# A recurrent attention feeding a gated MLP: attention one chunk ahead instead of two, second product two steps behind, a fixed activation table set with Ln ahead of the Exp, and an own order of units for the first three steps

## Chip, cores, metric

The kernel runs on one core of one Trainium2 chip. The metric is the device time of one execution in microseconds (us). The kernel before takes 262.17 us, the median of four runs (260.22 to 262.91).

## The reference

Gated linear attention over 768 positions (4 batches, 8 heads, head size 48), and its output as the input of an MLP whose gate is h·cos(h):

```python
for t in range(S):                                  # attention, per batch and head
    state = alpha[:, :, t, :, None] * state + einsum('bhd,bhe->bhde', k[:, :, t], v[:, :, t])
    y[:, :, t] = einsum('bhd,bhde->bhe', q[:, :, t], state)
x = y.transpose(0, 2, 1, 3).reshape(3072, 384)
h = x @ w_in                                        # 384 -> 2048, "ff1" below
out = (h * np.cos(h)) @ w_out                       # 2048 -> 384, "ff2" below
```

## The kernel before

The 3072 rows are worked through in 24 chunks of 128 rows (six per batch). The order of instructions on each engine is the order in which the program writes them; nothing reorders them afterwards. The decay is handled through logarithms: Ln of alpha, a cumulative sum on TensorE ("cums"), then two Exp. This is done for two chunks at a time. The cosine is a Sin with bias pi/2. Units, with the engine of each:

- Per pair of chunks: `ln` (ACT), `cums` (PE), `exps` (two Exp, ACT).
- Attention of a chunk: `operands` (GpSimd), `transposes` (PE, "T"), `ev_transposes` (DVE), `state` (PE, "S") and its eviction (DVE), `scores` (PE) and their masking (DVE), `outputs` (PE) and `ev_outputs` (DVE).
- MLP of a chunk, in two halves: `ff1` (PE), `act` (Sin, ACT), `gate` (multiply, DVE), `ff2` (PE), and the eviction of the result (ACT).

PSUM holds eight banks. Three two-bank buffers ("big") go round among ff1, scores and cums. One bank ("g") goes round among transposes, state and outputs, so each of these three waits until DVE has evicted the one before. One bank ("o") holds ff2's result.

```python
    def load_w1(f0, f1): ...
    def cast_w1(f0, f1):
        nc.scalar.activation(out=w1[:, 0:2, f0:f1], in_=w1f[:, 0:2, f0:f1], func=AF.Copy)
        nc.vector.tensor_copy(out=w1[:, 2, f0:f1], in_=w1f[:, 2, f0:f1])
    def cast_w2(f):
        nc.vector.tensor_copy(out=w2[:, f : f + 8], in_=w2f[:, f : f + 8])
    ...
    def prep(g):
        cums(2 * g, 2)
        exps(2 * g, 2)
        if 2 * g + 2 < NCH:
            ln(2 * g + 2, 2)

    nc.scalar.preload_act_table_set("natural_log_exp_and_others")
    load_a(0); load_qk(0); load_v(0); load_a(1)          # written on lines of their own
    load_w1(0, DF // 2)
    load_qk(1); load_v(1)
    load_w1(DF // 2, DF)
    load_a(2); load_a(3)
    ...                                                   # more loads; chunks 0 to 2 of the attention
    for s in range(NCH + 1):
        ...                                               # loads
        if s + 3 < NCH: operands(s + 3, nc.gpsimd)
        if s + 2 < NCH: transposes(s + 2); ev_transposes(s + 2)
        if s < NCH:     ff1(s, 0); t0 = act(s, 0)
        if s + 2 < NCH: state(s + 2); ev_state(s + 2)
        if s < NCH:     gate(s, 0, t0)
        if s == 0:      cast_w1(DF // 2, DF)
        if s == 1:      cast_w2(0); cast_w2(8)            # a loop in the source
        if s >= 1:      ff2(s - 1, 0)
        if s < NCH:     ff1(s, 1); t1 = act(s, 1)
        if s + 1 < NCH: outputs(s + 1); ev_outputs(s + 1)
        if s < NCH:     gate(s, 1, t1)
        if s >= 1:      ff2(s - 1, 1); ev_ff2(s - 1)
        if s + 2 < NCH: scores(s + 2); mask_scores(s + 2)
        if s % 2 == 0 and s + 4 < NCH:
            prep(s // 2 + 2)
```

## Time and profile before

| | before |
|---|---|
| time, median of four | 262.17 us |
| span of the profiled run | 260.2 us |
| PE busy | 211.3 us |
| ACT / DVE / GpSimd busy | 135.6 / 136.1 / 62.6 us |
| start of step 2 (its transposes) | 57.4 us |
| three pairs of steps, mean (103.42 to 159.64 us, between first matmuls of cums) | 18.74 us |

The page of the kernel before: the engines' busy time with share of the span and number of instructions, and the clock granted to TensorE in 40 slices of 6.5 us, in tenths.

```profile
PE 211.3 (81%) x2625; PEld 155.4 (60%) x2626; DVE 136.1 (52%) x160; ACT 135.6 (52%) x144; POOL 62.6 (24%) x104
...
PEclk9775779689999979999999999999999989999998
```

PE is the busiest engine, and it is idle 19% of the time. The clock is lower in most of the start (slices 2 to 9) and again in slices 15 and 33.

The timeline of the kernel before over one boundary of a pair. Columns: start in us, duration in us, engine, line, operation, output and input with shapes, count; in brackets the idle time of the engine before it and what ended it. L161 and L163 are the two Exp, L131 is Ln, L311 Sin, L316 the gate, L287 the eviction of the attention's outputs, L192 the transposes.

```profile
122.97 1.28 ACT L161 ACT_TABLE_LOAD   x1 [0.49 <-PE cum_new L148]
...
124.97 0.81 ACT L163 ACTIVATE cp_new<-cum_new 128x776 f32<-128x776 f32 x1
...
125.81 1.28 ACT L131 ACT_TABLE_LOAD   x1
...
127.10 0.84 ACT L131 ACTIVATE lnab<-a_new 128x768 bf16<-128x768 f32 x1
...
127.96 1.28 ACT L311 ACT_TABLE_LOAD   x1
...
129.25 2.12 ACT L311 ACTIVATE c_sb<-t,halfpi 128x1024 bf16<-128x1024 f32 x2
...
130.40 1.22 DVE L316 TENSOR_TENSOR g_new<-t,c_sb 128x1024 bf16<-128x1024 f32 x1 [4.70 <-ACT c_sb L311]
...
131.54 0.55 DVE L287 CAST t<-t 128x384 bf16<-128x384 f32 x1
...
132.14 0.38 PE L192 MATMUL t<-ident_bf,khb 128*128 128x128 bf16 x4 [1.55 <-DVE t L287]
```

Read it from top to bottom as one chain. After the cums ACT loads a table, does two Exp, loads a second table for Ln, does Ln, loads a third for Sin, and only then starts the Sin of an ff1 that PE had finished long before. The gate on DVE waits 4.70 us for it. The output eviction, whose input was ready, stands behind that gate in DVE's order, and PE's transposes wait 1.55 us for the bank that it frees.

The table of waits of the kernel before, PE only, 57 to 225 us: who waited for whom, total us, number, longest.

```profile
PE t L192 <- DVE t L287: 14.6, 8, 2.3
PE t L232 <- DVE t L198: 5.5, 6, 0.9
```

Both waits together are 20.1 us, which is all of PE's idle time in this stretch (168.0 us, PE busy 147.9). L232 is the state product, L198 the eviction of the transposes.

PE in the start of the kernel before:

```profile
27.46 2.64 PE L302 MATMUL t<-t,w_112 128*128 128x128 bf16 x24
...
49.91 2.72 PE L325 MATMUL o_new<-w_114,g_new 128*128 128x384 bf16 x8 [7.99 <-DVE w_114 L125]
...
57.41 0.40 PE L192 MATMUL t<-ident_bf,khb 128*128 128x128 bf16 x4
```

The first ff1 matmul (L302) runs at 27.46 us. The first ff2 matmul (L325) waits 7.99 us for the cast of w2. Step 2 starts at 57.41 us.

### The profile page before, as it was taken

The page shows a single profiled execution, that of the slowest core. Times are in us where ns is not written, and L with a number is a line of the kernel's source. Part 1 is how long each engine was busy: PE and PEld are TensorE (multiplying, and loading weights), DVE is VectorE, ACT ScalarE, POOL GpSimd, SP SyncE. Part 2 cuts the span into 40 slices and gives each one's busy share as a digit, 9 for nine tenths or more (in the row PEclk, how much of TensorE's full clock was granted, in tenths as well). Part 3 has the DMA queues.
Part 4 walks back from the last instruction along what each step waited for, and adds up shares of the span by engine and source line. Part 5 has one row for each costly group of instructions (what it writes and reads, how often), then busy time and mean ns, then how long its engine had stood idle before and what let it go on. Part 6 is the DMA issues. An engine that isn't in the chain of part 4 may idle for free. (4 is left out here: it accounts for less than half of the span.)

```text
span 260.2 us, 6131 instructions
## 1 busy us (share of the span) xinstructions
PE 211.3 (81%) x2625; PEld 155.4 (60%) x2626; DVE 136.1 (52%) x160; ACT 135.6 (52%) x144; POOL 62.6 (24%) x104
## 2 busy tenths in 40 slices
PE   7661673399969969969969869879789699999994
PEld 2430562176846856847747557567567487676762
DVE  6450234845465266276186185276366456765540
ACT  4323657123863943953944925916836736523440
POOL 3121215610420610610700700701602502500000
PEclk9775779689999979999999999999999989999998
DMA  8999999907734843743762671664355140000001
GB/s 142 314 300 188 347 238 179 197 5 154 152 74 84 155 99 53 154 107 60 141 133 59 115 151 41 113 146 93 69 123 116 39 92 33 33 2 31 33 30 62
DMA packets 106203, 30.28 MB, mean 116 GB/s; under 512 B 100288, under 2 KB 105408, under 8 KB 106176
## 3 DMA queue, kind: packets, MB, share of 16 engines
q1 hardware_dynamic: 106176, 29.89, 54.0%
q8 instruction: 20, 0.33, 0.5%
q14 instruction: 7, 0.06, 0.1%
HBM read 25.17 MB, written 4.72 MB: 115 GB/s over the span
## 5 line engine op out<-in xcount | busy, mean ns | idle before, releaser
L311 ACT ACTIVATE c_sb<-t,halfpi 128x1024 bf16<-128x1024 f32 x48 | 52.5, 1112 | 71.2 <-PE t L302 71.1
L316 DVE TENSOR_TENSOR g_new<-t,c_sb 128x1024 bf16<-128x1024 f32 x48 | 58.5, 1218 | 49.9 <-ACT c_sb L311 49.9
L302 PE MATMUL t<-t,w_112 128*128 128x128 bf16 x1152 | 77.4, 227 | 3.2 <-ACT w_112 L115 3.2
L325 PE MATMUL o_new<-w_114,g_new 128*128 128x384 bf16 x384 | 71.9, 332 | 8.6 <-DVE w_114 L125 8.0
L302 PEld LDWEIGHTS <-w_112 128*128 128x128 bf16 x1152 | 72.4, 103 | 6.9 <-ACT w_112 L115 3.5
L173 POOL TENSOR_TENSOR khb<-t,icp_new 128x384 bf16<-128x384 f32 x24 | 24.2, 1008 | 154.6 <-ACT icp_new L161 131.5
L325 PEld LDWEIGHTS <-g_new 128*128 128x128 bf16 x384 | 36.0, 99 | 32.0 <-issue 10.7
L287 DVE CAST t<-t 128x384 bf16<-128x384 f32 x24 | 13.3, 554 | 32.8 <-PE t L261 32.8
L218 DVE TENSOR_TENSOR t<-t,mask_f 128x1024 bf16<-128x1024 f32 x24 | 29.3, 1220 | 1.8 <-PE t L209 1.2
L244 DVE TENSOR_TENSOR t<-t,Em 128x384 bf16<-128x384 f32 x24 | 13.4, 558 | 21.1 <-PE t L238 18.9
L330 ACT ACTIVATE o_sb<-o_new 128x384 f32<-128x384 f32 x24 | 11.8, 490 | 23.3 <-PE o_new L325 23.3
L175 POOL TENSOR_TENSOR qhb<-t,cp_new 128x384 bf16<-128x384 f32 x22 | 23.4, 1062 | 0.6 <-DMA t<-in_q_dram 0.6
L192 PE MATMUL t<-ident_bf,khb 128*128 128x128 bf16 x96 | 9.6, 223 | 17.1 <-DVE t L287 14.6
L198 DVE COPY t<-t 128x1024 bf16<-128x1024 bf16 x24 | 16.4, 682 | 9.9 <-PE t L192 9.9
L261 PE MATMUL t<-t 128*64 128x128 bf16 (+1 forms) x160 | 20.8, 231 | 0.0
L261 PE MATMUL t<-t,vpb 128*64 128x128 bf16 x288 | 18.9, 228 | 0.7 <-DVE t L244 0.7
L131 ACT ACTIVATE lnab<-a_new 128x768 bf16<-128x768 f32 (+1 forms) x13 | 10.3, 794 | 14.7 <-DMA a_new<-in_alpha_dram 14.6
L192 PEld LDWEIGHTS <-khb 128*128 128x128 bf16 x96 | 6.4, 99 | 19.4 <-issue 14.7
L161 ACT ACT_TABLE_LOAD x10 | 12.8, 1283 | 4.5 <-PE cum_new L148 4.4
L261 PEld LDWEIGHTS <-t 128*64 128x64 bf16 (+1 forms) x160 | 10.4, 100 | 6.7 <-issue 0.2
L311 ACT ACT_TABLE_LOAD x11 | 14.1, 1283 | 0.2
L232 PE MATMUL t<-vpb,khb 128*128 128x96 bf16 x96 | 8.7, 216 | 6.7 <-DVE t L198 6.7
(44 smaller groups left out, 158.0 us busy)
## 6 DMA issues: line engine op xcount, KB each, us to landing
a_new<-in_alpha_dram SPq DMA_DIRECT2D x24, 192.0 KB, 3.5
t<-in_k_dram SPq DMA_DIRECT2D x24, 192.0 KB, 3.8
t<-in_q_dram SPq DMA_DIRECT2D x24, 192.0 KB, 4.1
t<-in_v_dram SPq DMA_DIRECT2D x24, 192.0 KB, 4.2
out_dram<-o_sb SPq DMA_DIRECT2D x24, 192.0 KB, 2.0
w1f<-in_moe_w_in_dram SPq DMA_DIRECT2D x2, 1536.0 KB, 8.0
w2f<-in_moe_w_out_dram SPq DMA_DIRECT2D x2, 1536.0 KB, 10.5
```

The costliest lines, as they stand in the source:

```text
L173: nc.gpsimd.tensor_tensor(out=khb[:, j % 3, :, 0:D], in0=k_sb, in1=icp.rearrange("s (h d) -> s h d", h=H), op=ALU.mult)
L175: qeng.tensor_tensor(out=qhb[:, j % 3, :, 0:D], in0=q_sb, in1=cp[:, 0:HD].rearrange("s (h d) -> s h d", h=H), op=ALU.mult)
L192: nc.tensor.transpose(t[:, (i * NP + p) * C : (i * NP + p + 1) * C], src[:, j % 3, 2 * p : 2 * p + 2].rearrange("s h d -> s (h d)"), ident_bf)
L198: nc.vector.tensor_copy(out=t, in_=qkT_ps.pop(j))
L218: nc.vector.tensor_tensor(out=t.rearrange("s (h t) -> s h t", h=H), in0=A_ps.pop(j).rearrange("s (h t) -> s h t", h=H), in1=mask_f.unsquee ...
L244: nc.vector.tensor_tensor(out=t.rearrange("r p (a e) -> r p a e", a=2), in0=U_ps.pop(j)[:, 0 : NP * 96].rearrange("r (p a e) -> r p a e", ...
L261: nc.tensor.matmul(t[r0 : r0 + n, kt * C : (kt + 1) * C], lhsT, rhs, start=start, stop=stop, skip_group_check=True)
L287: nc.vector.tensor_copy(out=t.rearrange("r k t -> r (k t)"), in_=y_ps.pop(j)[:, 0 : 3 * C])
L302: nc.tensor.matmul(t[:, f], w1[:, kk, ft * C : (ft + 1) * C], x_t[j][:, kk], start=(kk == 0), stop=(kk == 2))
L311: nc.scalar.activation(out=c_sb, in_=t, func=AF.Sin, bias=halfpi, scale=1.0)
L316: nc.vector.tensor_tensor(out=g_t[j][:, half * HF : (half + 1) * HF], in0=t, in1=c_sb, op=ALU.mult)
L325: nc.tensor.matmul(o_ps[j][:, 0:DM], g_t[j][:, ft], w2[:, ft], start=(ft == 0), stop=(ft == NF - 1))
```

## The change

Its intent: fewer table loads, Ln out of the way between Exp and Sin, attention only one chunk ahead so that the MLP can start earlier, ff2 two steps behind so that it never waits for a gate, casts split over ACT and DVE, and an order of units chosen by hand for steps 0 to 2. Letters stand for units; small letters are mostly the DVE or ACT part of the unit (`T` transposes, `t` their eviction, `S`/`u` state, `A`/`m` scores and mask, `Y`/`y` outputs, `0`/`1` ff1 halves, `i`/`j` Sin, `p`/`r` gates, `2`/`3` ff2 halves, `e` result, `o` operands, `C` cums, `x` Exp, `n` Ln, `P` explicit table load, `v` w1 cast, `a`/`b` w2 casts, `w` four warm-up matmuls).

```diff
 def cast_w1(f0, f1):
-    nc.scalar.activation(out=w1[:, 0:2, f0:f1], ...)      # ACT two thirds, DVE one third
-    nc.vector.tensor_copy(out=w1[:, 2, f0:f1], ...)
+    nc.vector.tensor_copy(out=w1[:, 0:2, f0:f1], ...)     # DVE two thirds, ACT one third
+    nc.scalar.activation(out=w1[:, 2, f0:f1], ...)
 def cast_w2(f):
-    nc.vector.tensor_copy(out=w2[:, f : f + 8], ...)
+    nc.vector.tensor_copy(out=w2[:, f : f + 5], ...)
+    nc.scalar.activation(out=w2[:, f + 5 : f + 8], ..., func=AF.Copy)
 ... # act/gate pass tiles through a dictionary; g_sb 4 buffers, c_sb 3
+def lnset():
+    nc.scalar.preload_act_table_set("natural_log_exp_and_others")
+def run(s, order):
+    g = (s + 3) // 2
+    ... # T..y work on chunk s+1, 0..r on s, 2 3 e on s-2, o on s+2, C x on pair g, n on pair g+1
 load_w1(0, DF // 2)
+load_a(2)
+load_a(3)
 load_qk(1)
 load_v(1)
 load_w1(DF // 2, DF)
-load_a(2)
-load_a(3)
 ... # two chunks fewer of alpha and one of q/k/v loaded ahead of the loop
-for s in range(NCH + 1):                    # the loop shown above
+for s in range(NCH + 2):
+    ... # loads
+    if s == 0:
+        run(0, "o 0i Tt Su Am p w Yy v")
+    elif s == 1:
+        run(1, "0i")
+        run(0, "1j r")
+        run(1, "o p Tt Su Am 1j r P")
+        ln(4, 2)
+        run(1, "C Yy x n")
+    elif s == 2:
+        run(2, "o Tt 0i Su Am a 1jp Yy r b 2 3 e")
+    elif s % 2 == 0:
+        run(s, "o Tt 0i Su Am 2 1j Yyp r 3 e")
+    else:
+        run(s, "o Tt 0i Su Am 2 1jp Yy r Pn 3 e C x")
```

More of the change, by code (lines that the diff above doesn't have):

```diff
@@ L114, in cast_w1 @@
     def cast_w1(f0, f1):
-        nc.scalar.activation(out=w1[:, 0:2, f0:f1], in_=w1f[:, 0:2, f0:f1], func=AF.Copy)
-        nc.vector.tensor_copy(out=w1[:, 2, f0:f1], in_=w1f[:, 2, f0:f1])
+        nc.vector.tensor_copy(out=w1[:, 0:2, f0:f1], in_=w1f[:, 0:2, f0:f1])
+        nc.scalar.activation(out=w1[:, 2, f0:f1], in_=w1f[:, 2, f0:f1], func=AF.Copy)
     def load_w2(f):
@@ L124, in cast_w2 @@
     def cast_w2(f):
-        nc.vector.tensor_copy(out=w2[:, f : f + 8], in_=w2f[:, f : f + 8])
+        nc.vector.tensor_copy(out=w2[:, f : f + 5], in_=w2f[:, f : f + 5])
+        nc.scalar.activation(out=w2[:, f + 5 : f + 8], in_=w2f[:, f + 5 : f + 8], func=AF.Copy)
     def ln(j0, n):
@@ L303, in ff1, with gate @@
                                  start=(kk == 0), stop=(kk == 2))
+    c_t = {}
     def act(j, half):
-        if half == 0:
-            g_new = moe.tile([C, NF, C], BF, tag="g_sb", bufs=3)
-            g_t[j] = g_new
-        t = h_ps.pop((j, half))
-        c_sb = moe.tile([C, HF, C], BF, tag="c_sb")
-        nc.scalar.activation(out=c_sb, in_=t, func=AF.Sin, bias=halfpi, scale=1.0)
-        return t, c_sb
-    def gate(j, half, tc_):
-        t, c_sb = tc_
-        nc.vector.tensor_tensor(out=g_t[j][:, half * HF : (half + 1) * HF], in0=t, in1=c_sb,
-                                op=ALU.mult)
+        c_sb = moe.tile([C, HF, C], BF, tag="c_sb", bufs=3)
+        nc.scalar.activation(out=c_sb, in_=h_ps[j, half], func=AF.Sin, bias=halfpi, scale=1.0)
+        c_t[j, half] = c_sb
+    def gate(j, half):
+        if j not in g_t:
+            g_new = moe.tile([C, NF, C], BF, tag="g_sb", bufs=4)
+            g_t[j] = g_new
+        nc.vector.tensor_tensor(out=g_t[j][:, half * HF : (half + 1) * HF],
+                                in0=h_ps.pop((j, half)), in1=c_t.pop((j, half)), op=ALU.mult)
     def ff2(j, half):
@@ L337, in warmup @@
             nc.tensor.matmul(w_ps, warm[:, 0:C], warm, start=True, stop=True)
-    def prep(g):
-        cums(2 * g, 2)
-        exps(2 * g, 2)
-        if 2 * g + 2 < NCH:
-            ln(2 * g + 2, 2)
-    nc.scalar.preload_act_table_set("natural_log_exp_and_others")
+    def lnset():
+        nc.scalar.preload_act_table_set("natural_log_exp_and_others")
+    def run(s, order):
+        g = (s + 3) // 2
+        units = {
+            "T": lambda: transposes(s + 1), "t": lambda: ev_transposes(s + 1),
+            "S": lambda: state(s + 1), "u": lambda: ev_state(s + 1),
+            "A": lambda: scores(s + 1), "m": lambda: mask_scores(s + 1),
+            "Y": lambda: outputs(s + 1), "y": lambda: ev_outputs(s + 1),
+            "0": lambda: ff1(s, 0), "1": lambda: ff1(s, 1),
+            "i": lambda: act(s, 0), "j": lambda: act(s, 1),
+            "p": lambda: gate(s, 0), "r": lambda: gate(s, 1),
+            "2": lambda: ff2(s - 2, 0), "3": lambda: ff2(s - 2, 1), "e": lambda: ev_ff2(s - 2),
+            "o": lambda: operands(s + 2, nc.gpsimd),
+            "C": lambda: cums(2 * g, 2), "x": lambda: exps(2 * g, 2),
+            "n": lambda: ln(2 * g + 2, 2), "P": lnset, "w": lambda: warmup(4),
+            "v": lambda: cast_w1(DF // 2, DF), "a": lambda: cast_w2(0), "b": lambda: cast_w2(8),
+        }
+        for c in order:
+            ahead = c in "TtSuAmYy"
+            if (
+                (ahead and s + 1 >= NCH) or (c in "01ijpr" and s >= NCH)
+                or (c in "23e" and s < 2) or (c == "o" and s + 2 >= NCH)
+                or (c in "Cx" and 2 * g >= NCH) or (c == "P" and 2 * g >= NCH)
+                or (c == "n" and 2 * g + 2 >= NCH) or c == " "
+            ):
+                continue
+            units[c]()
+    lnset()
     load_a(0)
@@ L365 @@
     load_v(3)
-    load_a(6)
-    load_a(7)
-    load_qk(4)
-    load_v(4)
     ln(0, 1)
@@ L377 @@
     warmup(4)
-    transposes(0)
-    ev_transposes(0)
+    run(-1, "Tt")
     cums(1, 1)
     exps(1, 1)
-    scores(0)
-    mask_scores(0)
-    warmup(4)
-    state(0)
-    ev_state(0)
-    outputs(0)
-    ev_outputs(0)
+    run(-1, "Amw Suw Yy")
     cast_w1(0, DF // 2)
+    ln(2, 2)
+    warmup(6)
+    cums(2, 2)
+    exps(2, 2)
     operands(1, nc.vector)
-    warmup(8)
-    transposes(1)
-    ev_transposes(1)
-    ln(2, 2)
-    state(1)
-    ev_state(1)
-    scores(1)
-    mask_scores(1)
@@ L399 @@
-    prep(1)
-    operands(2, nc.gpsimd)
-    for s in range(NCH + 1):
-        if s + 8 < NCH:
-            load_a(s + 8)
-        if s + 5 < NCH:
-            load_qk(s + 5)
-            load_v(s + 5)
-        if s + 3 < NCH:
-            operands(s + 3, nc.gpsimd)
-        if s + 2 < NCH:
-            transposes(s + 2)
-            ev_transposes(s + 2)
-        if s < NCH:
-            ff1(s, 0)
-            t0 = act(s, 0)
-        if s + 2 < NCH:
-            state(s + 2)
-            ev_state(s + 2)
-        if s < NCH:
-            gate(s, 0, t0)
-        if s == 0:
-            cast_w1(DF // 2, DF)
-        if s == 1:
-            for f in range(0, NF, 8):
-                cast_w2(f)
-        if s >= 1:
-            ff2(s - 1, 0)
-        if s < NCH:
-            ff1(s, 1)
-            t1 = act(s, 1)
-        if s + 1 < NCH:
-            outputs(s + 1)
-            ev_outputs(s + 1)
-        if s < NCH:
-            gate(s, 1, t1)
-        if s >= 1:
-            ff2(s - 1, 1)
-            ev_ff2(s - 1)
-        if s + 2 < NCH:
-            scores(s + 2)
-            mask_scores(s + 2)
-        if s % 2 == 0 and s + 4 < NCH:
-            prep(s // 2 + 2)
+    for s in range(NCH + 2):
+        for j in range(6 if s == 0 else s + 7, min(s + 8, NCH)):
+            load_a(j)
+        if s + 4 < NCH:
+            load_qk(s + 4)
+            load_v(s + 4)
+        if s == 0:
+            run(0, "o 0i Tt Su Am p w Yy v")
[11 more added lines that the diff above has]
+            run(s, "o Tt 0i Su Am 2 1jp Yy r Pn 3 e C x")
```

## The prediction

> **What bounds it now.** The engine table gives PE 211 us busy of a 260.2 us span, the others at most 136: PE is the engine to feed. Three parts:
> - Start (PE timeline: step 2 starts at 57.4 us). The first ff1 matmul is at 27.5 us, behind the operands of chunk 2, which wait for alpha 2/3 (landed at 22.3). PE idles 8.0 us at 42-50 for the w2 cast (DVE, 4.6 us), itself behind table loads, Ln waiting for alpha 6/7, and a Sin.
> - Steady state, 57 to 225 us: a pair of steps takes 18.6 us (122.2 to 140.8); its matmuls need about 16.1 (T 0.46, ff1 1.34+1.40, S 0.34, A 0.33, ff2 1.30+1.41, outputs 1.18 each step; cums 0.54). The loss is one chain: cums, Exp table load 1.28, two Exp 1.6, Ln load 1.28, Ln 0.84, Sin load 1.28, Sin 1.1; the gate waits 4.7 us for it, the output eviction stands behind the gate on DVE, and the next transposes wait for that eviction (waits: 14.6 us in 8), then S for theirs (6.7 in 8). The clock falls to 0.83-0.87 after it in two 10-us windows.
> - Tail: 3.8 us after the last matmul.
>
> **What the change does.** PE work stays, apart from six warm-up matmuls or so more.
> 1. Fixed table set: Exp and Ln share one load, two loads a pair instead of three: 1.28 us less on the ACT chain. The Trainium skill ("ScalarE: Activation LUTs", section "Table sets") says one set holds both; this trace shows three 1283 ns loads a pair. In the built order loads go from 31 to 22.
> 2. After the Exp/Ln batch the output eviction goes before the gates on DVE, so PE no longer waits for Sin; ff2, two steps behind, never waits for a gate. Laying the durations in order I find about 0.4 us of wait left per pair (S behind the transposes' eviction, as eviction, gate, gate, eviction run back to back). Pair 16.5 us: 2.1 less, times ten: 20 us, plus a few for the clock.
> 3. Start: alpha 2/3 come before q/k/v 1; ff1 of chunk 0 straight after the cums, at about 17 us; w1 cast mostly on DVE (about 1.4 us). Step 2 then starts at 42-45 us instead of 57.4, with one ff2 (2.7) and one T/S/A (1.1) less done. In step 2 the w2 casts (5/8 of 2.3 us each on DVE, between gates) cost about 3 us of PE wait.
> 4. Tail: two ff2 at the end with one output bank: 0.6 us more.
>
> Sum: step 2 at 43.5, remaining matmuls 179, pair stalls 4, w2 3.5, clock and unseen waits 4, end 4.5: span 238, time about 240 us.
>
> **Predicted: 240 us, 8 in 10 between 233 and 249.** Faster by over 2% 0.95, within 2% 0.04, slower 0.01.
>
> **What would show it.**
> - Pair 16.3-17.2 us; transposes' wait for the output eviction under 2 us in total; some wait of S for the transposes' eviction left.
> - Table loads 22; ACT 11 us or so less busy with them.
> - First ff1 at 16-19 us, step 2 at 41-47, first ff2 stopping between its halves for the second w2 cast.
> - Granted clock near 1.00 from 60 us on.
>
> **What would make it wrong.** Start: if inputs land later than in the old order (DMA share about 1.0 until 50 us), or PE runs at half clock through its gaps, step 2 starts near 50 and the time is 246-249. Steady state: if DVE's fixed order (gates behind an eviction that waits for PE) makes PE wait for the three two-bank buffers, the pair is 17.5 or more and half of the gain is gone. If ACT or POOL slip a step, the transposes wait for POOL instead.

## The result, and the profile after

| | before | after |
|---|---|---|
| time, median of four | 262.17 us | 234.56 us (234.29 to 237.25) |
| ratio after/before, 95% interval | | 0.8978 (0.8907 to 0.905) |
| span of the profiled run | 260.2 us | 235.5 us |
| PE busy | 211.3 us | 210.1 us |
| table loads in the built program | 31 | 22 |
| start of step 2 | 57.4 us | 42.6 us |
| three pairs of steps, mean | 18.74 us | 16.30 us |

A ratio here is the mean time of one kernel's runs over the mean of the other's of the same rounds, so it is not quite the ratio of the medians quoted. Executions over 1.5% slower than the fastest of the same kernel are left out of the means. The profiled run of the changed kernel is its slowest (237.25 us at a mean granted clock of 0.949; the others 234.3 to 234.9 at 0.963), so the traces show 24.7 us of difference where the medians show 27.6.

The same lines of the page, changed kernel:

```profile
PE 210.1 (89%) x2632; PEld 154.6 (66%) x2632; DVE 136.0 (58%) x160; ACT 124.7 (53%) x137; POOL 62.9 (27%) x104
...
PEclk9995985597999999999999999999999999999999
```

PE does nearly the same work in a shorter span, and its clock shows 9 (0.9 or more) from slice 11 on. ACT is 10.9 us less busy: it has nine table loads of 1.28 us fewer.

The boundary of a pair in the changed kernel, the same columns. Lines have moved by one or so: L348 is the explicit load, L132 Ln, L164 the second Exp, L310 Sin, L288 the output eviction, L317 the gate, L233 the state product.

```profile
129.09 1.28 ACT L348 ACT_TABLE_LOAD   x1
...
130.04 0.24 PE L149 MATMUL cum_new<-ones_bf,lnab 128*128 128x1 bf16 x4
...
130.38 0.84 ACT L132 ACTIVATE lnab<-a_new 128x768 bf16<-128x768 f32 x1
...
132.19 0.82 ACT L164 ACTIVATE cp_new<-cum_new 128x776 f32<-128x776 f32 x1
...
133.03 1.28 ACT L310 ACT_TABLE_LOAD   x1
...
134.33 2.33 ACT L310 ACTIVATE c_sb<-t,halfpi 128x1024 bf16<-128x1024 f32 x2
...
136.72 0.56 DVE L288 CAST t<-t 128x384 bf16<-128x384 f32 x1 [2.51 <-PE t L262]
...
137.20 2.35 DVE L317 TENSOR_TENSOR g_new<-t,c_sb 128x1024 bf16<-128x1024 f32 x2
...
140.20 0.34 PE L233 MATMUL t<-vpb,khb 128*128 128x96 bf16 x4 [0.32 <-DVE t L199]
```

The table load and Ln now stand before the Exp. Sin starts 4.1 us after the end of the cums (130.28 to 134.33), where before it started 6.4 us after (122.89 to 129.25). The row holds two Sin of 1.11 us each, so the first is done at about 135.4, before the outputs are; DVE, idle for 2.51 us, waits for PE's outputs at 136.72. PE's transposes have no wait. The state product still waits 0.32 us.

PE's waits in the changed kernel, 56 to 225 us:

```profile
PE t L233 <- DVE t L199: 2.9, 9, 0.3
```

20.1 us have become 2.9. The start of the changed kernel, PE (L303 ff1, L326 ff2, L145 cums, L193 transposes):

```profile
16.10 2.11 PE L303 MATMUL t<-t,w_112 128*128 128x128 bf16 x24
...
32.64 0.34 PE L233 MATMUL t<-vpb,khb 128*128 128x96 bf16 x4 [3.75 <-DVE t L199]
...
42.57 0.59 PE L193 MATMUL t<-ident_bf,khb 128*128 128x128 bf16 x4 [0.65 <-DVE t L288]
...
54.28 2.67 PE L326 MATMUL o_new<-w_114,g_new 128*128 128x384 bf16 x8 [2.33 <-DVE w_114 L125]
```

Where the 24.7 us of the traces lie can be read from the first matmul of the cums of chunks 6 and 7. It comes at 65.40 us before and at 65.03 after, 0.4 us apart; but the changed kernel has by then done one ff1 (2.7 us) and one set of outputs (1.2 us) more. The next eight pairs take 150.99 us before (65.40 to 216.39) and 130.06 after (65.03 to 195.09): 20.9 us. The rest to the end is 3.4 us shorter. So the start is worth about 4.3 us (0.4 + 3.9), the steady state 20.9, and the end costs about 0.5 us. Some 1.1 us of the steady state belong to the clock: two of the eight pairs of the kernel before took 19.39 and 19.33 us, with one ff1 at 2.49 and 2.77 us instead of 1.50 right after the wait.

The prediction's range holds the result. Its mechanism for the largest part, the order of eviction and gate on DVE, was only argued, and nothing above tests it: three things changed on that chain at once. The experiments take them apart.

### The profile page after: what moved, and what is told of

Same layout as the page of the kernel before. It is cut to its first block, busy times and chain, and to the rows that moved or that the text cites. A ratio compares the mean times of both kernels' runs of the same rounds, so it can differ in the third digit from the quotient of the medians.

```text
span 235.5 us, 6142 instructions
## 1 busy us (share of the span) xinstructions
PE 210.1 (89%) x2632; PEld 154.6 (66%) x2632; DVE 136.0 (58%) x160; ACT 124.7 (53%) x137; POOL 62.9 (27%) x104
## 4 chain that ended last, share of the span: by engine, by line
PE 70%; DVE 18%; DMA 4%; ACT 2%; SPq 2%; issue 2%; ACTq 0%
PE o_new L326 23%; PE t L303 22%; DVE g_new L317 11%; PE t L262 11%; DMA a_new<-in_alpha_dram 4%; PE t L210 3%; PE t L193 3%; DVE t L199 3%; DVE t L288 3%; PE t L233 3%; PE cum_new L145 2%; PE t L239 2%; DVE w_114 L125 1%; DVE w_112 L115 1%; PE w_ps L338 1%
## 5 line engine op out<-in xcount | busy, mean ns | idle before, releaser
L310 ACT ACTIVATE c_sb<-t,halfpi 128x1024 bf16<-128x1024 f32 x48 | 53.5, 1114 | 63.1 <-PE t L303 62.7
L303 PE MATMUL t<-t,w_112 128*128 128x128 bf16 x1152 | 75.1, 224 | 1.0 <-DVE t L288 0.7
L326 PE MATMUL o_new<-w_114,g_new 128*128 128x384 bf16 x384 | 71.5, 331 | 3.9 <-DVE w_114 L125 2.8
L303 PEld LDWEIGHTS <-w_112 128*128 128x128 bf16 x1152 | 69.8, 100 | 4.5 <-DVE t L288 0.8
L317 DVE TENSOR_TENSOR g_new<-t,c_sb 128x1024 bf16<-128x1024 f32 x48 | 57.5, 1216 | 7.6 <-ACT c_sb L310 7.2
L326 PEld LDWEIGHTS <-g_new 128*128 128x128 bf16 x384 | 34.5, 98 | 28.3 <-issue 5.4
L288 DVE CAST t<-t 128x384 bf16<-128x384 f32 x24 | 13.4, 557 | 41.9 <-PE t L262 41.9
L199 DVE COPY t<-t 128x1024 bf16<-128x1024 bf16 x24 | 16.5, 687 | 12.7 <-PE t L193 12.7
L176 POOL TENSOR_TENSOR qhb<-t,cp_new 128x384 bf16<-128x384 f32 x22 | 22.8, 1037 | 0.1
L233 PE MATMUL t<-vpb,khb 128*128 128x96 bf16 x96 | 8.5, 213 | 7.4 <-DVE t L199 7.4
L348 ACT ACT_TABLE_LOAD x11 | 14.1, 1283 | 0.9 <-PEq L448 0.7
L310 ACT ACT_TABLE_LOAD x11 | 14.1, 1283 | 0.2
L145 PE MATMUL cum_new<-lnab,triu_bf 128*128 128x384 bf16 x24 | 7.6, 343 | 7.3 <-ACT lnab L132 7.3
L132 ACT ACTIVATE lnab<-a_new 128x768 bf16<-128x768 f32 (+1 forms) x13 | 10.3, 793 | 6.4 <-DMA a_new<-in_alpha_dram 6.3
L178 POOL CAST vpb<-t 128x384 bf16<-128x384 f32 x24 | 13.1, 545 | 1.1 <-DMA t<-in_v_dram 0.6
## 6 DMA issues: line engine op xcount, KB each, us to landing
w2f<-in_moe_w_out_dram SPq DMA_DIRECT2D x2, 1536.0 KB, 10.9
```

The source lines that it names most:

```text
L176: qeng.tensor_tensor(out=qhb[:, j % 3, :, 0:D], in0=q_sb, in1=cp[:, 0:HD].rearrange("s (h d) -> s h d", h=H), op=ALU.mult)
L199: nc.vector.tensor_copy(out=t, in_=qkT_ps.pop(j))
L233: nc.tensor.matmul(t[:, p * 96 : (p + 1) * 96], khb[:, j % 3, 2 * p : 2 * p + 2].rearrange("s h d -> s (h d)"), vpb[:, j % 3, 2 * p : 2 * ...
L288: nc.vector.tensor_copy(out=t.rearrange("r k t -> r (k t)"), in_=y_ps.pop(j)[:, 0 : 3 * C])
L303: nc.tensor.matmul(t[:, f], w1[:, kk, ft * C : (ft + 1) * C], x_t[j][:, kk], start=(kk == 0), stop=(kk == 2))
L310: nc.scalar.activation(out=c_sb, in_=h_ps[j, half], func=AF.Sin, bias=halfpi, scale=1.0)
```

## The experiments

Theory A: the pair's loss hung on the length of the chain cums, Exp, Ln, Sin on ACT; cutting loads and moving Ln is what counts. Theory B, that of my prediction: it is the output eviction going before the gate on DVE. Each run was timed three rounds (the last one five) against the kernel before on the same chip, whose medians there were 261.4 to 262.0 us. "Pair" is the mean of three consecutive pairs, one of which holds the first chunk of a batch; pairs and waits are read from one profiled execution of each kernel. All results matched the reference.

### The short ACT chain in the old order

All edits below are cut to what differs. `b_set`: the kernel before, plus one line.

```diff
 def prep(g):
     cums(2 * g, 2)
+    nc.scalar.preload_act_table_set("natural_log_exp_and_others")
     exps(2 * g, 2)
```

> The kernel before with one thing changed: an explicit load of the set that holds both Exp and Ln ahead of each pair's two Exp, so Ln needs no load of its own (23 table loads instead of 31). Theory A (the Exp/Ln/Sin chain on ACT is what PE's wait hangs on, and the length of that chain is what the change cut): the chain is 1.28 us shorter plus up to 0.5 us because the explicit load does not stand behind the cums; gate, output eviction and transposes come 1.3 to 1.8 us earlier; a steady pair takes 16.8 to 17.4 us instead of 18.6, time 243 to 249 us. Theory B (my prediction's step 2: it is the order of eviction and gate on DVE that counts, the saved load is only 1.28 us off a chain that would still be hidden or still be waited for): the pair stays at 17.9 or above, time above 254 us.

Measured: 243.29 us, ratio 0.929 (0.925 to 0.934), pair 16.84 us. PE's wait for the output eviction fell from 14.6 to 1.1 us. One line gave 18.3 us (261.60 to 243.29), where the whole change gave 27.6, without a change of DVE's order. Theory A's ranges hold; theory B asked for a pair of 17.9 us and a time of 254 us or more. PE's waits, 57 to 225 us, and two lines of its timeline on ACT:

```profile
PE t L232 <- DVE t L198: 5.9, 8, 0.9
PE t L192 <- DVE t L287: 1.1, 3, 0.4
...
130.89 1.28 ACT L342 ACT_TABLE_LOAD   x1
...
135.75 2.12 ACT L311 ACTIVATE c_sb<-t,halfpi 128x1024 bf16<-128x1024 f32 x2
```

The state product's wait (L232) stays. The cums end at 131.29 us here; the load no longer waits for them, and Sin starts 4.5 us after their end instead of 6.4. The 1.9 us that the chain has lost are the 1.9 us that the pair has lost (18.74 to 16.84).

`b_set_ln`: the same, and Ln ahead of the Exp.

```diff
             ff2(s - 1, 1)
+            if s % 2 == 0 and s + 4 < NCH:
+                nc.scalar.preload_act_table_set("natural_log_exp_and_others")
+                if s + 6 < NCH:
+                    ln(s + 6, 2)
             ev_ff2(s - 1)
 # and in prep: exps as above; ln and the load there only for the first two pairs
```

> The same, and from step 2 on the load and the Ln of the next pair stand before the output eviction and the Exp, as in the changed kernel, not behind the Exp. DVE order, attention two ahead, ff2 one behind and the start stay as before. Theory A: chain after the cums another 2.1 us shorter (load 1.28, Ln 0.84), pair 16.3 to 16.8 us, time 240 to 246 us: the steady state of the changed kernel without its new order of units. Theory B: pair at least 17.3 us, time above 250 us.

Measured: 236.60 us, ratio 0.903 (0.898 to 0.908), pair 16.03 us, better than I expected. No wait of PE of the steady state is left in the table. Its boundary:

```profile
126.19 1.28 ACT L443 ACT_TABLE_LOAD   x1
...
128.31 0.24 PE L148 MATMUL cum_new<-ones_bf,lnab 128*128 128x1 bf16 x4
...
130.18 1.28 ACT L311 ACT_TABLE_LOAD   x1
...
131.48 1.11 ACT L311 ACTIVATE c_sb<-t,halfpi 128x1024 bf16<-128x1024 f32 x1
...
132.62 1.23 DVE L316 TENSOR_TENSOR g_new<-t,c_sb 128x1024 bf16<-128x1024 f32 x1 [1.27 <-ACT c_sb L311]
...
133.83 0.56 DVE L287 CAST t<-t 128x384 bf16<-128x384 f32 x1
```

Sin starts 2.9 us after the cums end (128.55 to 131.48). The gate is done in front of the output eviction, in the old order, and delays it hardly. Attention is still two ahead and ff2 one behind here, and the pair is shorter than the changed kernel's. So none of these, nor the new order of DVE, is needed for the fast steady state.

### The DVE order alone

`b_yfirst`: the kernel before, in odd steps the first gate behind the output eviction.

```diff
-        if s < NCH:
+        if s < NCH and s % 2 == 0:
             gate(s, 0, t0)
 ...
             ev_outputs(s + 1)
+        if s < NCH and s % 2 == 1:
+            gate(s, 0, t0)
```

> The kernel before with one thing changed: in the steps after an Exp/Ln batch the first gate stands behind the output eviction on DVE. Theory B: the wait of the transposes for the output eviction (14.6 us in all) goes, pair about 16.5 to 17.2 us, time 241 to 249 us. Theory A: the same late Sin now holds PE through the first gate (two-bank buffer of the next ff1) and through the transposes' eviction, which stands behind both gates and the mask: pair 17.7 to 18.4 us, time 252 to 261 us.

Measured: 254.09 us, ratio 0.967 (0.959 to 0.974), pair 18.27 us. The wait for the output eviction is gone, as theory B says, but two others grew in its place. PE's waits, 57 to 225 us:

```profile
PE t L232 <- DVE t L198: 11.9, 9, 1.4
PE t L302 <- DVE g_new L316: 6.4, 8, 1.3
```

The same late Sin holds PE through the gate, which frees ff1's buffer (L316, 6.4 us), and through the transposes' eviction, which queues behind the gates (11.9 us). Of the 7.1 us by which the two traces differ, 3.0 lie before the cums of chunks 6 and 7 (65.40 against 62.44 us) and 4.9 in the eight pairs after them. A wait that is moved is not a wait that is removed.

### Undoing single parts in the changed kernel

`a_gatefirst`: gate before eviction in even steps, as the odd steps have it.

```diff
-            run(s, "o Tt 0i Su Am 2 1j Yyp r 3 e")
+            run(s, "o Tt 0i Su Am 2 1jp Yy r 3 e")
```

> The changed kernel with the first gate before the output eviction in even steps, as in its odd steps. Theory A: Sin ends 1.2 us before the outputs do, so the gate fits in front for nothing, the transposes' eviction no longer queues behind two gates, and the 0.32 us wait of the state product goes: pair 16.2 to 16.4 us instead of 16.6, time 230.5 to 233 us. Theory B (eviction first is what removes PE's wait): pair 17.5 us or more, time above 242 us.

Measured: 230.03 us, ratio 0.880 (0.877 to 0.883), pair 15.80 us: faster than the changed kernel by about 4.5 us of the medians, and better than I expected in both figures. The lines that show it:

```profile
129.24 2.33 ACT L310 ACTIVATE c_sb<-t,halfpi 128x1024 bf16<-128x1024 f32 x2
...
130.39 1.23 DVE L317 TENSOR_TENSOR g_new<-t,c_sb 128x1024 bf16<-128x1024 f32 x1 [1.27 <-ACT c_sb L310]
...
131.64 0.56 DVE L288 CAST t<-t 128x384 bf16<-128x384 f32 x1
...
134.63 0.33 PE L233 MATMUL t<-vpb,khb 128*128 128x96 bf16 x4
```

The first gate runs in DVE's idle time before the outputs are ready; the state product (L233) has no wait. In the changed kernel the state product comes 1.83 us after the first matmul of the ff1 before it (138.37 to 140.20), here 1.34 us (133.29 to 134.63). So the order that I had called the cure costs 0.5 us a pair.

`a_threeloads`: from step 3 on no explicit table load.

```diff
-            run(s, "o Tt 0i Su Am 2 1jp Yy r Pn 3 e C x")
+            run(s, "o Tt 0i Su Am 2 1jp Yy r n 3 e C x")
```

> The changed kernel with one thing undone from step 3 on: no explicit table set, so Ln and Exp each load their own (30 loads instead of 22); Ln still stands before the Exp. Theory A laid out with durations: Sin of the even step ends 1.28 us later, at 136.7 on the changed kernel's clock of time, just when the output eviction starts; gates after that eviction are not held; pair 16.5 to 16.8 us as against 16.6, time within 2 us of the changed kernel (about 234.5). Rival (the table load itself is worth its 1.28 us per pair): pair 17.9 us, time about 246 us.

Measured: 235.61 us (233.46 to 235.95), ratio 0.899 (0.893 to 0.904), pair 16.46 us: not told apart from the changed kernel in time. With Ln in front and the eviction before the gates, the third load of 1.28 us is mostly hidden: one pair in three takes 17.08 us instead of 16.59, the others are as before. The saved load was worth much in the old order and next to nothing here.

`a_oldact`: the whole old order of ACT (no explicit load, Ln last). `a_oldact_gatefirst`: that, and gate first.

```diff
-            run(s, "o Tt 0i Su Am 2 1jp Yy r Pn 3 e C x")
+            run(s, "o Tt 0i Su Am 2 1jp Yy r 3 e C x n")
# a_oldact_gatefirst also:
-            run(s, "o Tt 0i Su Am 2 1j Yyp r 3 e")
+            run(s, "o Tt 0i Su Am 2 1jp Yy r 3 e")
```

> The changed kernel with the old ACT order from step 3 on: no explicit set, Exp first, then Ln with its own load, then Sin (30 loads); eviction before gates on DVE kept. Theory A: Sin of the even step 3.4 us later, first gate at about 138 and second at 139 on the changed kernel's clock of time; the first product of the next step waits 0.3 to 0.6 us for a bank, the state product 0.6 to 0.9 for the transposes' eviction: pair 17.0 to 17.4 us, time 239 to 243 us. Theory B: pair stays 16.6 to 16.8, time below 237 us.

> The old ACT order and the gate before the output eviction together, in the changed kernel. Both theories expect PE's wait for the output eviction to come back. Theory A: 1.3 to 2.2 us per pair, pair 17.9 to 18.6 us, time 248 to 255 us, so the two parts are not additive: either alone removes most of the wait. If the pair stays under 17.4 us, neither matters and the rest of the new order (one chunk ahead, ff2 two behind) is what counts.

Measured: `a_oldact` 239.73 us, ratio 0.918 (0.914 to 0.922), pair 16.90 us. The time is in theory A's range, the pair just below it. Of the two waits that theory A named, the state product's came, and the one for a bank did not:

```profile
PE t L233 <- DVE t L199: 7.7, 9, 0.9
```

`a_oldact_gatefirst` 241.59 us (median of three fast runs; a slow one took 243.93), ratio 0.924 (0.919 to 0.929), pair 17.41 us: a miss, over 6 us below the expected range, and at the 17.4 us under which I had written that neither part matters. The wait for the output eviction came back, as expected:

```profile
PE t L193 <- DVE t L288: 11.6, 8, 1.4
```

But it is 1.4 us a time and the pair is still 1.3 us shorter than before. In the kernel before the state product waits a further 0.92 us after it, because the mask product (1.22 us) stands between the gates and the transposes' eviction on DVE; in the new order of units the mask comes early in the step, and that wait doesn't appear in this run. I read that from the two traces; no run moves the mask alone, so this part stays argued. What the four kernels do show: with the short chain, eviction first loses 4.5 us (234.56 against 230.03, intervals apart). With the long chain it gains 0.5 us a pair in the traces (16.90 against 17.41); the medians differ by 1.9 us, and the intervals of the ratios overlap. And with both parts undone the changed kernel keeps 1.3 of the 2.4 us a pair that the change won, so the short chain is enough for the gain of the steady state (`b_set_ln`), but it isn't the only way to a part of it.

`a_ff2one`: ff2 one step behind.

```diff
-            "2": lambda: ff2(s - 2, 0), "3": lambda: ff2(s - 2, 1), "e": lambda: ev_ff2(s - 2),
+            "2": lambda: ff2(s - 1, 0), "3": lambda: ff2(s - 1, 1), "e": lambda: ev_ff2(s - 1),
 # step 2 does ff2 of chunks 0 and 1
```

> The changed kernel with the second product one step behind (both products of chunks 0 and 1 in step 2, from then on one behind), everything else kept. Theory: the gates of the step before are done 0.7 us or more before the second product wants them, so lag two buys nothing in the steady state; pair 16.6 us as before, one eviction wait of 0.58 us moves from the end to step 2; time 233.5 to 236 us. Rival (the extra step of lag is what hides the late gates): pair 17 us or more, time above 238 us.

Measured: 233.73 us, ratio 0.892 (0.888 to 0.896), pair 16.29 us. The second step of lag buys nothing that can be seen; 0.8 us in its disfavour is within the spread.

### The start

`a_oldloads`: the changed kernel with alpha 2 and 3 loaded where they were.

```diff
-    load_a(2)
-    load_a(3)
     load_qk(1)
     load_v(1)
     load_w1(DF // 2, DF)
+    load_a(2)
+    load_a(3)
```

> The changed kernel with alpha of chunks 2 and 3 loaded behind q/k/v 1 and the second half of w1, as before. Theory S (the earlier alpha load is what frees the start): the Ln of chunks 2/3 moves from 14.7 to about 22 us, the first ff1 matmul from 16.1 to about 24 us, step 2 from 42.6 to 46-49 us; time 238 to 242 us. Rival (the start is bound elsewhere, by the DVE chain of step 1 and the DMA queue, and absorbs it): first ff1 late, but step 2 within 2 us of the changed kernel's and time below 237 us.

Measured: 242.14 us, ratio 0.923 (0.918 to 0.928). The first ff1 and the transposes of step 2, PE:

```profile
24.01 2.72 PE L303 MATMUL t<-t,w 128*128 128x128 bf16 x24
...
50.21 0.58 PE L193 MATMUL t<-ident_bf,khb 128*128 128x128 bf16 x4 [0.65 <-DVE t L288]
```

Both come 7.6 to 7.9 us later than in the changed kernel (16.10 and 42.57), and the time is 7.6 us longer, just past the upper end of what I expected; nothing absorbs the delay. In the new order the first ff1 stands behind the cums of this Ln, so the place of two 192 KB loads in the queue is worth more than the whole net gain of the start.

`b_set_ln_loads`: the same two loads moved, but in the old order of units with the short ACT chain.

```diff
+    load_a(2)
+    load_a(3)
     load_qk(1)
     load_v(1)
     load_w1(DF // 2, DF)
-    load_a(2)
-    load_a(3)
```

> The old order of units with the short ACT chain (the run at 236.6 us), and the new load order on top. Theory: load order alone does nothing for the old order of units, because its first ff1 stands behind the operands of chunk 2 (k lands at about 24 us) and its w2 casts behind a Sin that waits for the Ln of chunks 6/7 (DMA lands at about 41 us): ff2's first matmul stays at 46-48 us, time 235 to 237.5 us. Rival: load order alone gives the start's gain, 230 to 233 us.

Measured: 237.65 us, ratio 0.907 (0.903 to 0.911), against 236.60 without and 235 to 237.5 expected: no gain. First ff1 and first ff2, PE:

```profile
26.77 2.77 PE L302 MATMUL t<-t,w 128*128 128x128 bf16 x24
...
48.26 2.72 PE L325 MATMUL o_new<-w,g_new 128*128 128x384 bf16 x8 [4.66 <-DVE w L125]
```

They stay about where they were in `b_set_ln` (27.41 and 47.40 us), behind the operands of chunk 2 and the w2 cast. Load order and order of units are worth something only together. No run undoes the split of the casts alone, so its share of the start isn't known.

`a_start`: gate first, and steps 1 to 3 arranged by the waits in the changed kernel's start (3.75 us at 32.64, 2.33 us at 54.28, and Sin of step 2 behind a Ln that waits for its DMA).

```diff
         elif s == 1:
             run(1, "0i")
-            run(0, "1j r")
-            run(1, "o p Tt Su Am 1j r P")
+            run(0, "1j")
+            run(1, "o Tt p Su Am")
+            run(0, "r")
+            run(1, "1j r P")
             ln(4, 2)
-            run(1, "C Yy x n")
+            run(1, "C Yy x a")
         elif s == 2:
-            run(2, "o Tt 0i Su Am a 1jp Yy r b 2 3 e")
+            run(2, "o 0i b Tt Su Am 1jp Yy r 2 3 e")
+        elif s == 3:
+            run(3, "o Tt 0i Su Am 2 1jp Yy r P")
+            ln(6, 2)
+            run(3, "n 3 e C x")
```

> Gate before eviction in even steps (the run at 230.0 us), and step 1 to 3 arranged by the waits that the changed kernel's trace shows: transposes of chunk 2 evicted before the gates of chunks 0 and 1 (PE waited 3.7 us), the first w2 cast in step 1's idle DVE time and the second at the head of step 2 (PE waited 0.4 and 2.3 us), Ln of chunks 6/7 moved to step 3 so that Sin of step 2 does not wait for its DMA. Theory: those waits lie on the critical path of the start; about 4 to 6 us less: time 224 to 227 us, start of step 3 at 47-49 us instead of about 53. Rival (the start is bound by the input DMA, chunk 3's k/q/v landing at about 38-40 us): within 2 us of 230.0.

Measured: 226.77 us, ratio 0.866 (0.862 to 0.871), pair 15.80 us as in `a_gatefirst`, step 3 from 50.05 us. The time is in the expected range; step 3 starts later than the 47 to 49 us I expected, and the gain over `a_gatefirst` is 3.3 us, not 4 to 6. PE:

```profile
26.98 0.34 PE L233 MATMUL t<-vpb,khb 128*128 128x96 bf16 x4 [0.79 <-DVE t L199]
...
36.02 2.72 PE L303 MATMUL t<-t,w 128*128 128x128 bf16 x24 [0.65 <-DVE t L288]
39.34 0.61 PE L193 MATMUL t<-ident_bf,khb 128*128 128x128 bf16 x4 [0.61 <-POOL khb L174]
...
47.44 2.77 PE L326 MATMUL o_new<-w,g_new 128*128 128x384 bf16 x16
```

The wait of the state product fell to 0.79 us, and ff2 of chunk 0 runs in one piece (sixteen matmuls at 47.44). New is a wait for GpSimd at 39.34: the operands of chunk 3, whose k has just landed.

`a_final`: that, ff2 one behind, and warm-up matmuls in two waits (`"www C Yy x a"` in step 1, `"o 0i b w Tt ..."` in step 2).

> The run at 226.8 us (gate before eviction, start rearranged) with two things on top: the second product one step behind, which took 0.8 us off the changed kernel, and warm-up matmuls in two waits of step 1 and 2 (twelve before the cums, where PE idles 3.4 us and the clock then halves: ff1 of step 2 took 2.72 and 2.74 us instead of 1.50; four before the transposes). Theory: ff1 of step 2 at about 1.5 us, the ff1 second half no longer late, input DMA of chunk 3 (about 38 us) left as the bound of step 2: time 222.5 to 225.5 us, granted clock 0.98 or more. Rival (the cold matmuls were hidden behind the operands of chunk 3): 225.5 to 227 us.

Measured, five rounds: 225.07 us (median of five fast runs, 224.60 to 227.37; a slow one took 228.69), ratio 0.862 (0.858 to 0.866). It is not told apart from `a_start`, and the time does not decide between theory and rival: the median lies in the theory's range, that of all six runs (225.81) in the rival's. The trace says more. The warm-ups did their work and it bought little here:

```profile
36.25 1.50 PE L303 MATMUL t<-t,w 128*128 128x128 bf16 x24 [0.65 <-DVE t L288]
...
39.98 0.40 PE L193 MATMUL t<-ident_bf,khb 128*128 128x128 bf16 x4 [1.37 <-POOL khb L174]
```

ff1 of step 2 takes 1.50 us instead of 2.72, and then PE waits for GpSimd longer (1.37 us). The transposes come no earlier than in `a_start` (39.98 against 39.34 us): up to this point the cold matmuls were hidden behind the operands of chunk 3, as the rival said. `a_start` and `a_final` beat both kernels, by 13 to 14% against the kernel before and by 3 to 4% against the changed one (ratios of the medians).

## Why the prediction was right or wrong, point by point

- What bounds the kernel: right. PE's two waits were 20.1 us; the changed kernel has 2.9.
- Step 1, table loads 31 to 22: right in number. I took 1.28 us a pair for its value. In the old order an explicit load is worth 1.9 us a pair (18.74 to 16.84), more than its own duration, because the load that it replaces also stood behind the cums (ACT idle 0.49 us before it, 122.97). In the new order it was worth next to nothing.
- Step 2 is the one whose mechanism failed: "After the Exp/Ln batch the output eviction goes before the gates on DVE, so PE no longer waits for Sin". The size was right (predicted 16.5 us, measured 16.59 twice and 15.70 in the pair with a batch's first chunk), the reason wrong. That the size held is luck in part: my own count of PE's matmuls was 16.1 us a pair, and once the wait is gone, by whatever means, the pair falls to about that. The old DVE order with a short chain has no such wait (`b_set_ln`), the new DVE order with the long chain gains 7.5 us (`b_yfirst`) where the one line of `b_set` gains 18.3, and undoing it in the changed kernel gains 4.5 us (`a_gatefirst`). I had not compared when Sin and the outputs are ready: with the short chain the first Sin is done at about 135.4 us in the trace shown, the outputs at about 136.6, so the gate could have gone first. I had also left out that Ln and its load go in front of the Exp, the second half of the shortening. My 0.4 us of wait for S per pair was right (0.32 in the table of waits, 0.49 by the start of the state product) and was the price of this order.
- "ff2, two steps behind, never waits for a gate": true, and of no use; with one step it doesn't either (`a_ff2one`).
- Step 3, the start: right. First ff1 at 16.1 us, step 2 at 42.6, ff2 split in step 2 with 0.41 and 2.33 us of wait. `a_oldloads` shows the dependence on alpha's DMA.
- Step 4, the end: two waits of ff2 for its bank, 1.2 us in all against 0.6, as predicted.
- The 5.4 us between 240 and 234.56: about 2.7 us is the profiled execution, which was that much slower than the other runs; about 2.7 us is the term "remaining matmuls 179", in which every chunk carried a state. The first chunk of a batch has none, and its pair takes 15.70 us instead of 16.59; three such pairs lie in the steady state (3 × 0.89 us). The wait of the kernel before had hidden this: its pairs took 18.6 to 18.8 us either way, except the two that the clock slowed. This sum is an estimate: step 2 (42.6 us against 43.5) and the w2 casts (2.7 against 3.5) came out nearly 1 us better each than I had put them, so something that I did not find took as much back.

Where the skill was used: "ScalarE: Activation LUTs", section "Table sets", says that one set holds Ln and Exp; the traces agree once the set is asked for by name. "TensorE: Matmul & The Clock Gate", Part 1, says that PE's clock halves after an idle window of about 3.4 us; in `a_start` ff1 took 2.72 us instead of 1.50 after the idle stretch of 3.36 us that ends at 33 us, and warm-ups in that stretch prevented it in `a_final`. One stretch of the changed kernel's start fits a conflict that "SBUF — State Buffer", section "Who interferes with whom", describes (a cast on DVE and a GpSimd operation can block each other): the first w2 cast took 1.92 us beside GpSimd's multiplies, one of which took 1.85 us instead of 1.00; the second cast, the same size with GpSimd idle, took 1.15 us. No run was made to test it.

What stays open: how the 1.3 us a pair between `a_oldact_gatefirst` (17.41) and the kernel before (18.74) divide among the mask's place, one chunk ahead, and the rest of the new order, and what the split casts are worth in the start.

## What to carry to other kernels

When an in-order engine waits for a late input, first ask how late the input is and shorten its chain; changing what stands behind the wait can leave most of it to the next buffer (`b_yfirst`). Ask for a table set by name where two functions share one, and put work that nobody waits for (here Ln of the next pair) in front of the wait, not behind it. After a change has removed a wait, test again the parts that were meant to dodge it: an order that helps with the late input can cost time with the early one.

## What the Trainium skill lacked or had wrong

- "ScalarE: Activation LUTs", section "Table sets", counts one load for Ln then Exp. The built programs loaded a set for each of the two when it was not named, in either order: 31 loads before (Exp first), 30 in `a_oldact` (Exp first) and in `a_threeloads` (Ln first), which name it up to step 1 only, and 22 or 23 where it is named each time. That a named load can be placed ahead of a wait, and that this was worth more than the load's 1.28 us (1.9 us a pair), is not there.
- The same page, section "What ACT_TABLE_LOAD costs", gives 1283 ns and a further drain of about 1380 ns for each switch. The 1283 ns are in the trace; the drain is not: a load at 133.03 us, right after an Exp that ended at 133.01, was followed by Sin at 134.33, so 1.3 us for the switch.
- "TensorE: Matmul & The Clock Gate", Part 1, names an idle window of about 3.4 us. Under "A second HAM failure mode" it lets frequent shorter idles swing the clock too, but gives no length for them. In the kernel before, the clock fell after two of the three waits of about 2.28 us: the next ff1 took 2.77 us after the wait that ended at 206.99 us and 2.49 us after the one that ended at 93.95, but 1.50 us after the one that ended at 150.77.
